# A decode block on one core: q, gate and up with x stationary in four column groups, and a new first and last DMA

## The chip, the core and the metric

The kernel runs on one core of a Trainium2 chip. The core has TensorE (PE, with its weight loads counted apart as PEld), VectorE (DVE), ScalarE (ACT), GpSimd (POOL) and SyncE (SP, which issues almost all DMAs here). The metric is the device time of one execution in microseconds (us). Three timed runs of the kernel before gave 197.55, 197.69 and 197.55 us, median 197.55.

## What is computed

One decode step of a gated mix of two branches that share the input x (4 rows of 512, bfloat16). Branch A is attention over the last 4096 positions of a cache, branch B is a gated feed-forward layer, and g is a scalar gate per row:

```python
g = sigmoid((x * gate_w).sum(-1, keepdims=True))
# A: 4 sequences, 32 query heads, 8 key/value heads of 128, window W = 4096 of 16384
q = (x @ wq).reshape(4, 1, 32, 128).transpose(0, 2, 1, 3)
k = repeat(k_cache[:, :, -4096:, :], 4, axis=1)        # v in the same way
p = softmax(einsum("bhqd,bhkd->bhqk", q, k) * 128 ** -0.5)
a = einsum("bhqk,bhkd->bhqd", p, v).reshape(4, 1, 4096) @ wo
# B: 512 -> 1792 -> 512
gate, up = x @ W_gate, x @ W_up
b = ((gate * (gate > 0)) * up) @ W_down
out = g * a + (1 - g) * b
```

All weights and caches are bfloat16. The window of both caches is 64 MB, wq and wo are 4 MB each, and the three matrices of B 1.75 MB each, so about 81 MB have to be read.

## The kernel before

The work on the cache is cut into eight sets (NSET): set s is sequence s // 2 and one half (four) of its key/value heads. A set's keys are one DMA of 4 MB into one of two buffers of Ksb (`load_k`, L235), its values one of 4 MB into one of two buffers of Vsb (`load_v`, L239). All big loads stand on SP's queue in one fixed order: wq, keys 0, then keys s and values s - 1 alternating, W_gate and W_up into the buffer that keys 6 leave free, values 7, W_down into the buffer of values 6, and wo in four pieces of 16, 10, 4 and 2 blocks (WO_CUTS) into the buffer that wq had. A load into a used buffer waits on SP for the last product that reads it, and all loads behind it wait with it. x and gate_w are two small loads on ACT's queue.

For a set, PE first transposes the keys in 16 groups of four 128x128 float32 blocks (two bfloat16 values as one; `kt`, L340), through three banks of PSUM (TR); each group is copied back to SBUF in bfloat16 by ACT (L345, nine of 16 groups) or DVE (L347). Then come the scores (`scores`, L373), with the query as the stationary operand of 32 columns and 512 keys as the moving one, in four column groups of the PE array, through three banks (SCB); DVE masks each bank of 512 columns and takes the maximum (L381). `maximum` reduces the maxima, `exponent` (ACT, L410) forms the weights, `turn` (DVE, L417) transposes them, `values` (PE, L429) multiplies them with the values into bank OB, whose result DVE copies to osb (L434); `combine` (PE, L442 and L445, then DVE to L450) adds the parts of the four column groups into bank FB, divides, multiplies by g and writes the set's columns of oq.

Every engine runs a list of operations in an order that is written out by hand (from L489). The class Program counts, for each operation, which semaphore values it has to wait for, and `emit` (L107) writes each engine's list into its own part of one `nc.Block()` (L562). For PE, sets 2 to 7 are three turns of a loop over one body of two sets. Block entry is a jump of every engine into its part; at its end the engines meet in a barrier.

The parts around the change. `qproj` (L454) runs first on PE, when wq has landed: for each of 32 heads, four products with a 128x128 block of wq stationary and the four columns of xT moving, into columns of FB; DVE casts the result (L461), two products with the matrices perm (made on POOL, L270) bring even and odd elements of a head apart (L464), and DVE spreads them into QS (L468), from which POOL copies a set's query to QSP (L357). `gateup` (L472) stands behind the exponents, `combine` of set 6 and the transpositions of set 7, and ahead of `values` of set 7: for each of 14 blocks of 128 and each of gate and up four products with a block of the weight stationary and xT moving (L477), into columns of FB; then three DVE operations (L481 to L483) form hT with the factor 1 - g. Last, PE multiplies hT with W_down (L545) and oq with wo (L553), both into bank AB in four column groups of 128 output columns; DVE copies AB to outs (L557), SP issues the DMA of the result, four rows of 128 columns from each of four places in outs (L558), and waits for it within the block (L559; the profile puts that wait at L562).

Of the kernel before, what the change touches and what calls it, by code (L numbers as in the profile page):

```python
# [5 lines left out]
FP32 = mybir.dt.float32  # L6
BF16 = mybir.dt.bfloat16
ACTF = mybir.ActivationFunctionType
ALU = mybir.AluOpType
# [4 lines left out]
HQ = 32  # L14
# [5 lines left out]
NSET = 8  # L20
NFT = FF // 128
# [12 lines left out]
class Program:  # L34
# [69 lines left out]
            if name is not None:  # L104
                ins.then_inc(sems[self.events[name][0]], step)

    def emit(self, engine, eng, sems):  # L107
        ops, plan = self.ops[engine], self.plan(engine)
        if engine != "pe":
            for op, need in zip(ops, plan):  # L110
                self.put(eng, sems, op, need)
            return
        n = len(self.turns) - 1
        base = []
# [38 lines left out]
def bass_gated_mix__sliding_block_cached__glu_gated_reglu__decode_kernel(  # L153
# [13 lines left out]
    with ExitStack() as ctx:  # L167
        def sb(name, shape, dt):
            return ctx.enter_context(nc.sbuf_tensor(name, shape, dt))
# [18 lines left out]
        qTb = sb("qTb", [128, 128], BF16)  # L188
        perm = sb("perm", [128, 2, 128], BF16)
# [15 lines left out]
        gtmp = sb("gtmp", [128, NFT * 4], FP32)  # L205
        gtmp2 = sb("gtmp2", [128, NFT * 4], FP32)
        hT = sb("hT", [128, NFT, 32], BF16)
        outs = sb("outs", [128, 128], BF16)
# [48 lines left out]
        wo_src = A_wo.rearrange("(p i) w -> p (i w)", p=128)  # L257
        for k in range(len(WO_CUTS) - 1):
            lo, hi = 512 * WO_CUTS[k], 512 * WO_CUTS[k + 1]
            P.dma("sp", lambda e, lo=lo, hi=hi: e.dma_start(Wbig[:, lo:hi], wo_src[:, lo:hi]), ("WO", k), [("Q",)])  # L260


        P.op("pool", lambda e: e.memset(ones[:, :], 1.0), ("ONES",))
# [5 lines left out]
        for h in range(2):  # L269
            P.op("pool", lambda e, h=h: e.affine_select(  # L270
                perm[:, h, :].rearrange("p (g k) -> p g k", g=2), ones[:, :].rearrange("p (g k) -> p g k", g=2),
                [[0, 2], [-2, 64]], ALU.is_equal, 0.0, base=-h, channel_multiplier=1), ("PERM", h), [("ONES",)])
        P.op("pool", lambda e: e.memset(m4[:, :], -NEG), ("M4Z",))
        for a in range(4):
            r = slice(32 * a, 32 * a + 32)
# [19 lines left out]
            ("WSUM",), [("S32", 3), ("WSEL", 3)])  # L295
        P.op("dve", lambda e: e.memset(QS[:, :, :].rearrange("p s w -> p (s w)"), 0.0), ("QZ",))
        P.op("dve", lambda e: e.memset(mcol[:, :], 0.0))
        P.op("dve", lambda e: e.memset(oq[:, :, :].rearrange("p i w -> p (i w)"), 0.0), ("OQZ",))
        P.op("dve", lambda e: e.memset(hT[:, :, :].rearrange("p i w -> p (i w)"), 0.0), ("HZ",))
        P.op("dve", lambda e: e.memset(mrow2[:, :], 0.0), ("M0",))  # L300
# [4 lines left out]
        for t in range(4):  # L305
# [2 lines left out]
        P.op("dve", lambda e: e.tensor_copy(xT[:, :].rearrange("p (t r) -> p t r", t=4)[:, :, 0:5],  # L308
                                            fbf[:, 0:32].rearrange("p (t r) -> p t r", t=4)[:, :, 0:5]),
             ("XTC",), [("XT",)])  # L310
        P.op("dve", lambda e: e.tensor_copy(gwB[:, :].rearrange("p (t m) -> p t m", t=4),
                                            xT[:, :].rearrange("p (t r) -> p t r", t=4)[:, :, 4:5].to_broadcast([128, 4, 128])),
             ("GWB",), [("XTC",)])
# [123 lines left out]
        def combine(s):  # L437
            par, b, half = s % 2, s // 2, s % 2
            r = slice(64 * half, 64 * half + 64)
            for k in range(8):  # L440
                lo = 3 - k % 4 + 64 * (k // 4)
                P.op("pe", lambda e, k=k, lo=lo: e.matmul(FB[r, 256:288], Wsel[:, lo:lo + 64], osb[:, par, 32 * k:32 * k + 32],  # L442
                                                          start=(k == 0), stop=(k == 7)), None,
                     [("OSB", s), ("WSUM",), ("QC", 1), ("G",), ("OQ", s - 1) if s >= 1 else None, ("H",) if s == NSET - 1 else None])
            P.op("pe", lambda e: e.matmul(FB[r, 288:288 + NPIECE], Wsum[:, :], rowsum[:, par, :], start=True, stop=True),  # L445
                 ("SUMS", s))
            P.op("dve", lambda e: e.tensor_reduce(ssum[r, par:par + 1], FB[r, 288:288 + NPIECE], AXIS.X, ALU.add),
                 ("SSUM", s), [("SUMS", s)])
            P.op("dve", lambda e: e.reciprocal(recip[r, par:par + 1], ssum[r, par:par + 1]), ("RECIP", s), [("SSUM", s)])
            P.op("dve", lambda e: e.tensor_scalar(oq[r, :, 8 * b], FB[r, 256:288], recip[r, par:par + 1],  # L450
                                                  gsb[r, b:b + 1], op0=ALU.mult, op1=ALU.mult),
                 ("OQ", s), [("RECIP", s), ("G",), ("OQZ",)])

        def qproj():  # L454
            for h in range(HQ):
                for t in range(4):
                    P.op("pe", lambda e, h=h, t=t: e.matmul(  # L457
                        FB[:, 64 + 4 * h:68 + 4 * h], Wq3[:, t, 128 * h:128 * h + 128], xT[:, t * 8:t * 8 + 4],
                        start=(t == 0), stop=(t == 3)),
                        ("Q",) if (h == HQ - 1 and t == 3) else None, [("WQ",), ("XTC",), ("G",)])  # L460
            P.op("dve", lambda e: e.tensor_copy(qTb[:, :].rearrange("p (b h) -> p b h", b=4),  # L461
                                                FB[:, 64:192].rearrange("p (h b) -> p b h", b=4)), ("QB",), [("Q",)])
            for h in range(2):
                P.op("pe", lambda e, h=h: e.matmul(OB[:, 128 * h:128 * h + 128], perm[:, h, :], qTb[:, :], start=True, stop=True),  # L464
                     ("QP",) if h == 1 else None, [("QB",), ("PERM", 1)])
            for g in range(2):
                r = slice(64 * g, 64 * g + 64)
                P.op("dve", lambda e, g=g, r=r: e.tensor_copy(  # L468
                    QS[r, :, 16 * g:16 * g + 16], OB[r, 0:256].rearrange("p (s j) -> p s j", j=16)),
                    ("QC", g), [("QP",), ("QZ",)])  # L470

        def gateup():  # L472
            for i in range(NFT):
                for which, W, key in ((0, Wg, "WG"), (1, Wu, "WU")):
                    col = 64 + 64 * which + 4 * i
                    for t in range(4):
                        P.op("pe", lambda e, W=W, i=i, t=t, col=col: e.matmul(  # L477
                            FB[:, col:col + 4], W[:, t, i:i + NFT * 127 + 1:NFT], xT[:, t * 8:t * 8 + 4],
                            start=(t == 0), stop=(t == 3)),
                            ("GU",) if (i == NFT - 1 and which == 1 and t == 3) else None, [("WG",), ("WU",), ("OQ", NSET - 2)])  # L480
            P.op("dve", lambda e: e.tensor_scalar(gtmp[:, :], FB[:, 64:64 + NFT * 4], 0.0, None, op0=ALU.max), ("H0",), [("GU",)])  # L481
            P.op("dve", lambda e: e.tensor_tensor(gtmp2[:, :], FB[:, 128:128 + NFT * 4], gtmp[:, :], ALU.mult), ("H1",), [("H0",)])
            P.op("dve", lambda e: e.tensor_tensor(  # L483
                hT[:, :, :].rearrange("p i (b o) -> p i b o", o=8)[:, :, :, 0], gtmp2[:, :].rearrange("p (i b) -> p i b", b=4),
                gsb[:, 4:8].rearrange("p (o b) -> p o b", o=1).to_broadcast([128, NFT, 4]), ALU.mult), ("H",),
                [("H1",), ("G",), ("HZ",)])


        qproj()  # L489
# [59 lines left out]
        for k in range(len(WO_CUTS) - 1):  # L549
            for i in range(WO_CUTS[k], WO_CUTS[k + 1]):  # L550
                for cb in range(4):
# [5 lines left out]
        P.op("dve", lambda e: e.tensor_copy(outs[:, :], AB[:, 0:128]), ("OUTS",), [("ACC",)])  # L557
        P.dma("sp", lambda e: e.dma_start(out.rearrange("b o (c d) -> c (b o) d", d=128), outs[0:128:8, :]), ("OUT",), [("OUTS",)])  # L558
        P.op("sp", None, None, [("OUT",)])  # L559

        sems = {name: ctx.enter_context(nc.semaphore(name)) for name in P.sems}
        with nc.Block() as block:  # L562
            @block.sync
            def _(e):
                P.emit("sp", e, sems)

            @block.gpsimd
            def _(e):
                P.emit("pool", e, sems)

            @block.tensor
            def _(e):
                P.emit("pe", e, sems)

            @block.vector
            def _(e):
                P.emit("dve", e, sems)

            @block.scalar
            def _(e):  # L580
                P.emit("act", e, sems)


# [26 lines left out]
```

## Time and profile before

The profiled execution took 197.38 us; its span, from the first to the last recorded instruction, is 195.7 us, and the mean granted clock of PE is 0.889 of full speed.

| | us in the span | share |
|---|---|---|
| PE products | 140.6 | 72% |
| PE weight loads | 107.7 | 55% |
| DVE | 103.6 | 53% |
| ACT | 91.5 | 47% |
| POOL | 7.9 | 4% |
| packets on SP's DMA queue (share of 16 DMA engines) | | 96.8% |

How the lines of the profile are read: a line of the chain has its start, its length and what it is; the chain is followed back from the end to what released each step. A line of the timeline has start, length, engine, line of the program, operation, the tiles written and read, the count of merged instructions, and in brackets the idle time ahead of it and what ended it. A line of the waits tells who waited for whom, in total, how often, and the longest. A line of a group has shortest, median and longest duration in nanoseconds, then first and last start. The forty digits are the busy share in forty equal slices of the span, in tenths. A line of the windows has the stretch and its length, the busy time of PE, PEld, DVE, ACT and POOL with the number of instructions, the granted clock of PE, the share of the 16 DMA engines that were busy, and GB/s.

### The profile page before, as it was taken

The numbers are of one execution on the slowest core, as the hardware profiler recorded it, in microseconds if no ns is written. First come the engines' busy times: TensorE is split into PE (matmuls) and PEld (weight loads), VectorE is DVE, ScalarE is ACT, GpSimd is POOL, SyncE is SP. The second block draws the span as 40 slices with busy tenths as digits, with TensorE's granted clock in tenths as the row PEclk, the third lists the DMA queues.
The fourth block names the chain that finished last, engine by engine and source line by source line (L and its number), as shares of the span: only waits on it lengthen the run. The fifth ranks groups of instructions, "written<-read, shape, count | busy, mean of one in ns | idle before, by whom it ended". The sixth has DMA issues, their size and how long they took to land.

```text
span 195.7 us, 4263 instructions
## 1 busy us (share of the span) xinstructions
PE 140.6 (72%) x1858; PEld 107.7 (55%) x1858; DVE 103.6 (53%) x278; ACT 91.5 (47%) x108; POOL 7.9 (4%) x39
## 2 busy tenths in 40 slices
PE   0134199968889919992999399929992999498634
PEld 0034197535567518751976286528752875397533
DVE  2102025888599456945585659456945584741200
ACT  2000058698398409760886098509750976220000
POOL 7400000000000000000000000000000000000000
PEclk9999999999999996997599879996996699965855
DMA  6999999999999999999999999999999999999991
GB/s 215 449 429 452 429 449 442 425 429 437 432 422 429 425 429 429 427 429 425 435 429 435 429 429 430 429 429 429 429 429 429 435 411 425 450 431 415 422 385 59
DMA packets 3498, 81.19 MB, mean 415 GB/s; under 512 B 409, under 2 KB 414, under 8 KB 670
## 3 DMA queue, kind: packets, MB, share of 16 engines
q1 hardware_dynamic: 3476, 81.01, 96.8%
q8 instruction: 9, 0.15, 0.3%
q14 instruction: 3, 0.02, 0.0%
q10 hardware_dynamic: 10, 0.01, 0.0%
HBM read 81.01 MB, written 0.00 MB: 414 GB/s over the span
## 4 chain that ended last, share of the span: by engine, by line
DMA 57%; PE 25%; ACT 9%; DVE 4%; issue 1%; SPq 1%
DMA Ksb<-in_A_k_cache_dram 46%; PE bank L340 16%; DMA Wbig<-in_A_wo_dram 12%; ACT Ksb L345 7%; PE bank L373 5%; DVE Ksb L347 2%; PE bank L429 2%; ACT sc L410 2%; PE bank L553 1%; PE bank L442 1%; DVE pT L417 1%; ACT L410 1%; DVE sc L381 1%; SPq L260 0%; DVE oq L450 0%
## 5 line engine op out<-in xcount | busy, mean ns | idle before, releaser
L345 ACT ACTIVATE Ksb<-bank 128x1024 bf16<-128x1024 bf16 x72 | 70.9, 1022 | 68.2 <-PE bank L340 68.0
L340 PE MATMUL bank<-identf,Ksb 128*128 128x128 f32 x512 | 81.1, 313 | 29.4 <-DMA Ksb<-in_A_k_cache_dram 24.0
L340 PEld LDWEIGHTS bank<-identf,Ksb 128*128 128x128 f32 x512 | 66.6, 161 | 44.1 <-DMA Ksb<-in_A_k_cache_dram 25.7
L347 DVE COPY Ksb<-bank 128x1024 bf16<-128x1024 bf16 x56 | 38.0, 685 | 41.8 <-PE bank L340 40.8
L381 DVE CUSTOM_DVE_ANT_0 sc<-bank,mask 128x512 bf16<-128x512 f32 x32 | 21.7, 684 | 9.6 <-PE bank L373 9.5
L429 PE MATMUL bank<-Vsb,pT 128*32 128x256 bf16 x512 | 20.8, 291 | 0.9 <-DMA Vsb<-in_A_v_cache_dram 0.9
L373 PE MATMUL bank<-Ksb,QSP 128*32 128x512 bf16 x256 | 19.4, 383 | 2.1 <-DVE Ksb L347 1.6
L410 ACT ACTIVATE sc<-sc,negmax 128x1024 bf16<-128x1024 bf16 x16 | 18.3, 1146 | 4.8 <-DVE negmax L402 4.7
L417 DVE STREAM_TRANSPOSE pT<-sc 128x1024 bf16<-128x1024 bf16 x16 | 19.7, 1237 | 1.3 <-ACT sc L410 1.0
L429 PEld LDWEIGHTS bank<-Vsb,pT 128*32 128x32 bf16 x512 | 13.2, 101 | 7.1 <-issue 3.3
L442 PEld LDWEIGHTS bank<-osb,Wsel 128*64 128x64 f32 x128 | 8.1, 138 | 4.6 <-issue 2.6
L442 PE MATMUL bank<-osb,Wsel 128*64 128x32 f32 x128 | 8.9, 224 | 1.2 <-DVE osb L434 1.2
L373 PEld LDWEIGHTS bank<-Ksb,QSP 128*32 128x32 bf16 x256 | 4.1, 94 | 9.4 <-DVE Ksb L347 4.4
L477 PE MATMUL bank<-xT,Ksb 128*128 128x4 bf16 x112 | 6.9, 199 | 1.8 <-DVE oq L450 1.8
L477 PEld LDWEIGHTS bank<-xT,Ksb 128*128 128x128 bf16 x112 | 6.8, 160 | 1.9 <-issue 1.9
L553 PE MATMUL bank<-Wbig,oq 128*32 128x128 bf16 x128 | 4.2, 311 | 4.1 <-DMA Wbig<-in_A_wo_dram 4.0
L357 POOL COPY QSP<-QS 128x64 bf16<-128x64 bf16 x8 | 1.8, 236 | 118.2 <-PE bank L373 107.4
L457 PE MATMUL bank<-xT,Wbig 128*128 128x4 bf16 x128 | 3.6, 166 | 4.0 <-DMA Wbig<-in_A_wq_dram 4.0
L306 PE MATMUL bank<-ident,xsb 5*128 5x5 bf16 x4 | 0.3, 167 | 7.9 <-DMA xsb<-in_gate_w_dram 7.9
L553 PEld LDWEIGHTS bank<-Wbig,oq 128*32 128x32 bf16 x128 | 3.1, 140 | 5.0 <-DMA Wbig<-in_A_wo_dram 5.0
L457 PEld LDWEIGHTS bank<-xT,Wbig 128*128 128x128 bf16 x128 | 3.5, 104 | 4.0 <-DMA Wbig<-in_A_wq_dram 4.0
L434 DVE COPY osb<-bank 128x256 f32<-128x256 f32 x8 | 3.4, 420 | 3.6 <-PE bank L429 3.6
(55 smaller groups left out, 47.0 us busy)
## 6 DMA issues: line engine op xcount, KB each, us to landing
Ksb<-in_A_k_cache_dram SPq DMA_DIRECT2D x8, 4096.0 KB, 22.9
Vsb<-in_A_v_cache_dram SPq DMA_DIRECT2D x8, 4096.0 KB, 32.0
Wbig<-in_A_wq_dram SPq DMA_DIRECT2D x1, 4096.0 KB, 12.2
Wbig<-in_A_wo_dram SPq DMA_DIRECT2D x1, 2048.0 KB, 20.2
Ksb<-in_B_W_gate_dram SPq DMA_DIRECT2D x1, 1792.0 KB, 17.9
Ksb<-in_B_W_up_dram SPq DMA_DIRECT2D x1, 1792.0 KB, 21.8
Vsb<-in_B_W_down_dram SPq DMA_DIRECT2D x1, 1792.0 KB, 15.6
Wbig<-in_A_wo_dram SPq DMA_DIRECT2D x1, 1280.0 KB, 22.8
```

The costliest lines, as they stand in the source:

```text
L340: P.op("pe", lambda e, bk=bk, cc=cc, c=c, s=s: e.transpose(bk[:, cc * 128:(cc + 1) * 128], kw[:, c * 128:(c + 1) * 128], identf[:, :]), (" ...
L345: P.op("act", lambda e: e.activation(dst, bk[:, :].bitcast(BF16), ACTF.Copy), ("KTC", s, i), [("KT", s, i)])
L347: P.op("dve", lambda e: e.tensor_copy(dst, bk[:, :].bitcast(BF16)), ("KTC", s, i), [("KT", s, i)])
L373: P.op("pe", lambda e, a=a, h=h: e.matmul(bk[32 * a:32 * a + 32, 0:512], QSP[:, s % 2, h, :], k4[:, 16 * bank:16 * bank + 16, 32 * a:32 * ...
L381: P.op("dve", lambda e: e.tensor_tensor_reduce(sc[:, s % 2, bank * 512:(bank + 1) * 512], bk[:, :], mask[:, :], 1.0, LOWEST, ALU.add, ALU.max,
L410: P.op("act", lambda e: e.activation(sc[:, par, k * PW:(k + 1) * PW], sc[:, par, k * PW:(k + 1) * PW], ACTF.Exp, bias=negmax[:, par:par + ...
L417: P.op("dve", lambda e: e.transpose(pT[:, par, k * PW:(k + 1) * PW], sc[:, par, k * PW:(k + 1) * PW]), ("PTT", s, k), [("EXP", s, k), ("PV ...
L429: P.op("pe", lambda e, c=c, g=g, col=col: e.matmul(OB[32 * g:32 * g + 32, 0:256], pT[:, par, col:col + 32], v3[:, 16 * k + c, :], start=(k ...
L442: P.op("pe", lambda e, k=k, lo=lo: e.matmul(FB[r, 256:288], Wsel[:, lo:lo + 64], osb[:, par, 32 * k:32 * k + 32], start=(k == 0), stop=(k ...
L457: P.op("pe", lambda e, h=h, t=t: e.matmul(FB[:, 64 + 4 * h:68 + 4 * h], Wq3[:, t, 128 * h:128 * h + 128], xT[:, t * 8:t * 8 + 4], start=(t ...
L477: P.op("pe", lambda e, W=W, i=i, t=t, col=col: e.matmul(FB[:, col:col + 4], W[:, t, i:i + NFT * 127 + 1:NFT], xT[:, t * 8:t * 8 + 4], star ...
L553: P.op("pe", lambda e, i=i, cb=cb: e.matmul(AB[32 * cb:32 * cb + 32, 0:128], oq[:, i, :], Wo3[:, i, cb * 128:(cb + 1) * 128], start=False, ...
```

## The change

- The first DMA of SP (wq) is issued ahead of the block, and SP's last operation, the wait for the result's DMA, behind it. `emit` gets bounds lo and hi for that.
- q: xP holds xT's four columns of x beside 28 zero columns, for each quarter t of the contraction. Each product has xP stationary (32 columns) and 512 columns of wq moving, in four column groups: 32 products into two banks of SCB. DVE copies the first bank twice into qdup, ACT the second; 16 products with qdup stationary and four columns of the identity moving bring q into the old layout in OB. The matrices perm go.
- gate and up: in the same way, 448 columns a group, 16 products each into two banks of TR; three passes and a transposition of 32x32 blocks on DVE form hT. PE waits for the banks of TR, no longer for FB, and `combine` of the last set no longer waits for H.
- A row of the result sits in rows 0 to 3 of a column group, no longer in every eighth row. Four copies (two on DVE, two on ACT) put the groups beside each other in outs, 4 rows of 512, and the result's DMA is a plain one of four rows.

```diff
-    def emit(self, engine, eng, sems):
+    def emit(self, engine, eng, sems, lo=0, hi=None):
...
-            for op, need in zip(ops, plan):
+            for op, need in list(zip(ops, plan))[lo:hi]:
...
+        P.op("dve", lambda e: e.tensor_copy(xP[:, :, 0:4], xT[:, :].rearrange("p (t r) -> p t r", t=4)[:, :, 0:4]),
+             ("XP",), [("XTC",), ("XZ",)])
...
-                     [("OSB", s), ("WSUM",), ("QC", 1), ("G",), ("OQ", s - 1) if s >= 1 else None, ("H",) if s == NSET - 1 else None])
+                     [("OSB", s), ("WSUM",), ("QC", 1), ("G",), ("OQ", s - 1) if s >= 1 else None])
...
         def qproj():
-            for h in range(HQ):
+            for n in range(2):
                 for t in range(4):
-                    P.op("pe", lambda e, h=h, t=t: e.matmul(
-                        FB[:, 64 + 4 * h:68 + 4 * h], Wq3[:, t, 128 * h:128 * h + 128], xT[:, t * 8:t * 8 + 4],
-                        start=(t == 0), stop=(t == 3)),
...
+                    for g in range(4):
+                        j = 4 * n + g
+                        P.op("pe", lambda e, n=n, t=t, g=g, j=j: e.matmul(
+                            SCB[n][32 * g:32 * g + 32, 0:512], xP[:, t, :], Wq3[:, t, 512 * j:512 * j + 512],
+                            start=(t == 0), stop=(t == 3), tile_position=(0, 32 * g)),
+                            ("Q", n) if (t == 3 and g == 3) else None, [("WQ",), ("XP",), ("G",)])
+            for n in range(2):
+                src = SCB[n][:, :].rearrange("p (m k c) -> p m c k", m=4, c=2)
+                for o in range(2):
+                    if n == 0:
+                        P.op("dve", lambda e, n=n, o=o, src=src: e.tensor_copy(qdup[:, n, :, :, o, :], src),
+                             ("QB", n, o), [("Q", n)])
+                    else:
+                        P.op("act", lambda e, n=n, o=o, src=src: e.activation(qdup[:, n, :, :, o, :], src, ACTF.Copy),
+                             ("QB", n, o), [("Q", n)])
...
+                        P.op("pe", lambda e, n=n, c=c, m=m: e.matmul(
+                            to[:, c, :, n, :, m], qdup[:, n, m, c, :, :].rearrange("p o k -> p (o k)"), of_b,
+                            start=True, stop=True),
...
         def gateup():
-            for i in range(NFT):
-                for which, W, key in ((0, Wg, "WG"), (1, Wu, "WU")):
...
+            for bank, W, key in ((TR[0], Wg, "WG"), (TR[1], Wu, "WU")):
+                for t in range(4):
+                    for g in range(4):
+                        P.op("pe", lambda e, bank=bank, W=W, t=t, g=g: e.matmul(
+                            bank[32 * g:32 * g + 32, 0:448], xP[:, t, :], W[:, t, 448 * g:448 * g + 448],
+                            start=(t == 0), stop=(t == 3), tile_position=(0, 32 * g)),
+                            ("GU", key) if (t == 3 and g == 3) else None,
+                            [(key,), ("KTC", NSET - 1, 14), ("KTC", NSET - 1, 15)])
...
+            P.op("dve", lambda e: e.transpose(gtmp3[:, :, :].rearrange("p i l -> p (i l)"),
+                                              gtmp2[:, :, :].rearrange("p i l -> p (i l)")), ("H2",), [("H1",)])
...
-        P.op("dve", lambda e: e.tensor_copy(outs[:, :], AB[:, 0:128]), ("OUTS",), [("ACC",)])
-        P.dma("sp", lambda e: e.dma_start(out.rearrange("b o (c d) -> c (b o) d", d=128), outs[0:128:8, :]), ("OUT",), [("OUTS",)])
+        for c in range(4):
+            to, src = outs[0:4, 128 * c:128 * c + 128], AB[32 * c:32 * c + 4, 0:128]
+            if c % 2 == 0:
+                P.op("dve", lambda e, to=to, src=src: e.tensor_copy(to, src), ("OUTS", c), [("ACC",)])
+            else:
+                P.op("act", lambda e, to=to, src=src: e.activation(to, src, ACTF.Copy), ("OUTS", c), [("ACC",)])
+        P.dma("sp", lambda e: e.dma_start(out.rearrange("b o d -> (b o) d"), outs[:, :]), ("OUT",), [("OUTS", c) for c in range(4)])
...
+        P.emit("sp", nc.sync, sems, 0, 1)
         with nc.Block() as block:
             @block.sync
             def _(e):
-                P.emit("sp", e, sems)
+                P.emit("sp", e, sems, 1, -1)
...
+        P.emit("sp", nc.sync, sems, -1)
```

More of the change, by code (lines that the diff above doesn't have):

```diff
@@ L187, in bass_gated_mix__sliding_block_cached__glu_gated_reglu__decode_kernel @@
         gsb = sb("gsb", [128, 8], FP32)
-        qTb = sb("qTb", [128, 128], BF16)
-        perm = sb("perm", [128, 2, 128], BF16)
+        qdup = sb("qdup", [128, 2, 4, 2, 2, 64], BF16)
+        xP = sb("xP", [128, 4, 32], BF16)
         QS = sb("QS", [128, 2 * NSET, 32], BF16)
@@ L204, in bass_gated_mix__sliding_block_cached__glu_gated_reglu__decode_kernel @@
         oq = sb("oq", [128, 32, 32], BF16)
-        gtmp = sb("gtmp", [128, NFT * 4], FP32)
-        gtmp2 = sb("gtmp2", [128, NFT * 4], FP32)
+        gtmp = sb("gtmp", [128, 32, NFT], FP32)
+        gtmp2 = sb("gtmp2", [128, NFT, 32], FP32)
+        gtmp3 = sb("gtmp3", [128, NFT, 32], FP32)
         hT = sb("hT", [128, NFT, 32], BF16)
-        outs = sb("outs", [128, 128], BF16)
+        outs = sb("outs", [4, 512], BF16)
         banks = [ctx.enter_context(nc.psum_tensor("bank%d" % i, [128, 512], FP32)) for i in range(8)]
@@ L259, in bass_gated_mix__sliding_block_cached__glu_gated_reglu__decode_kernel @@
             lo, hi = 512 * WO_CUTS[k], 512 * WO_CUTS[k + 1]
-            P.dma("sp", lambda e, lo=lo, hi=hi: e.dma_start(Wbig[:, lo:hi], wo_src[:, lo:hi]), ("WO", k), [("Q",)])
+            P.dma("sp", lambda e, lo=lo, hi=hi: e.dma_start(Wbig[:, lo:hi], wo_src[:, lo:hi]), ("WO", k), [("Q", 1)])
         P.op("pool", lambda e: e.memset(ones[:, :], 1.0), ("ONES",))
@@ L268, in bass_gated_mix__sliding_block_cached__glu_gated_reglu__decode_kernel @@
                                                base=0, channel_multiplier=1), ("IDENTF",), [("ONESF",)])
[L269 to L272, printed above, removed]
         P.op("pool", lambda e: e.memset(m4[:, :], -NEG), ("M4Z",))
@@ L297, in bass_gated_mix__sliding_block_cached__glu_gated_reglu__decode_kernel @@
         P.op("dve", lambda e: e.memset(mcol[:, :], 0.0))
+        P.op("dve", lambda e: e.memset(xP[:, :, :].rearrange("p t w -> p (t w)"), 0.0), ("XZ",))
         P.op("dve", lambda e: e.memset(oq[:, :, :].rearrange("p i w -> p (i w)"), 0.0), ("OQZ",))
@@ L449, in combine @@
             P.op("dve", lambda e: e.reciprocal(recip[r, par:par + 1], ssum[r, par:par + 1]), ("RECIP", s), [("SSUM", s)])
-            P.op("dve", lambda e: e.tensor_scalar(oq[r, :, 8 * b], FB[r, 256:288], recip[r, par:par + 1],
+            P.op("dve", lambda e: e.tensor_scalar(oq[r, :, b], FB[r, 256:288], recip[r, par:par + 1],
                                                   gsb[r, b:b + 1], op0=ALU.mult, op1=ALU.mult),
@@ L454, in qproj @@
         def qproj():
-            for h in range(HQ):
+            for n in range(2):
                 for t in range(4):
-                    P.op("pe", lambda e, h=h, t=t: e.matmul(
-                        FB[:, 64 + 4 * h:68 + 4 * h], Wq3[:, t, 128 * h:128 * h + 128], xT[:, t * 8:t * 8 + 4],
-                        start=(t == 0), stop=(t == 3)),
-                        ("Q",) if (h == HQ - 1 and t == 3) else None, [("WQ",), ("XTC",), ("G",)])
-            P.op("dve", lambda e: e.tensor_copy(qTb[:, :].rearrange("p (b h) -> p b h", b=4),
-                                                FB[:, 64:192].rearrange("p (h b) -> p b h", b=4)), ("QB",), [("Q",)])
@@ L463, in qproj @@
-            for h in range(2):
-                P.op("pe", lambda e, h=h: e.matmul(OB[:, 128 * h:128 * h + 128], perm[:, h, :], qTb[:, :], start=True, stop=True),
-                     ("QP",) if h == 1 else None, [("QB",), ("PERM", 1)])
+                    for g in range(4):
[4 more added lines that the diff above has]
+                            ("Q", n) if (t == 3 and g == 3) else None, [("WQ",), ("XP",), ("G",)])
@@ new lines, in qproj @@
+            of_b = ident[:, :].rearrange("p (g w) -> p w g", g=4)[:, 0:4, :]
+            to = OB[:, 0:256].rearrange("p (c b n g m) -> p c b n g m", c=2, b=4, n=2, g=4)
+            for n in range(2):
+                for c in range(2):
+                    for m in range(4):
+                        P.op("pe", lambda e, n=n, c=c, m=m: e.matmul(
+                            to[:, c, :, n, :, m], qdup[:, n, m, c, :, :].rearrange("p o k -> p (o k)"), of_b,
+                            start=True, stop=True),
+                            ("QP",) if (n, c, m) == (1, 1, 3) else None, [("QB", n, 1), ("IDENT",)])
@@ L472, in gateup @@
         def gateup():
-            for i in range(NFT):
-                for which, W, key in ((0, Wg, "WG"), (1, Wu, "WU")):
[L475 to L480, printed above, removed]
@@ L481, in gateup @@
-            P.op("dve", lambda e: e.tensor_scalar(gtmp[:, :], FB[:, 64:64 + NFT * 4], 0.0, None, op0=ALU.max), ("H0",), [("GU",)])
-            P.op("dve", lambda e: e.tensor_tensor(gtmp2[:, :], FB[:, 128:128 + NFT * 4], gtmp[:, :], ALU.mult), ("H1",), [("H0",)])
-            P.op("dve", lambda e: e.tensor_tensor(
-                hT[:, :, :].rearrange("p i (b o) -> p i b o", o=8)[:, :, :, 0], gtmp2[:, :].rearrange("p (i b) -> p i b", b=4),
-                gsb[:, 4:8].rearrange("p (o b) -> p o b", o=1).to_broadcast([128, NFT, 4]), ALU.mult), ("H",),
-                [("H1",), ("G",), ("HZ",)])
+            for bank, W, key in ((TR[0], Wg, "WG"), (TR[1], Wu, "WU")):
[6 more added lines that the diff above has]
+                            [(key,), ("KTC", NSET - 1, 14), ("KTC", NSET - 1, 15)])
@@ new lines, in gateup @@
+            P.op("dve", lambda e: e.tensor_scalar(gtmp[:, :, :].rearrange("p l i -> p (l i)"), TR[0][:, 0:448], 0.0, None,
+                                                  op0=ALU.max), ("H0",), [("GU", "WG")])
+            P.op("dve", lambda e: e.tensor_tensor(
+                gtmp2[:, :, :].rearrange("p i l -> p l i"), TR[1][:, 0:448].rearrange("p (l i) -> p l i", i=NFT),
+                gtmp[:, :, :], ALU.mult), ("H1",), [("H0",), ("GU", "WU")])
+            P.op("dve", lambda e: e.transpose(gtmp3[:, :, :].rearrange("p i l -> p (i l)"),
+                                              gtmp2[:, :, :].rearrange("p i l -> p (i l)")), ("H2",), [("H1",)])
@@ L489, in bass_gated_mix__sliding_block_cached__glu_gated_reglu__decode_kernel @@
+            P.op("dve", lambda e: e.tensor_tensor(
+                hT[:, :, 0:4], gtmp3[:, :, 0:4], gsb[:, 4:8].rearrange("p (o b) -> p o b", o=1).to_broadcast([128, NFT, 4]),
+                ALU.mult), ("H",), [("H2",), ("G",), ("HZ",)])
         qproj()
```

## The prediction

> **What bounds the kernel now.** I read the page's forty slices first, then the queue shares, the chain, and the two ends.
>
> ```profile
> DMA  6999999999999999999999999999999999999991
> q1 hardware_dynamic: 3476, 81.01, 96.8%
> q8 instruction: 9, 0.15, 0.3%
> HBM read 81.01 MB, written 0.00 MB: 414 GB/s over the span
> ```
>
> The 16 DMA engines are full in every slice but the first and last. Nothing that only shortens an engine's work in the middle can pay. The last pieces of the chain agree:
>
> ```profile
> 168.06 22.77 DMA Wbig<-in_A_wo_dram
> 190.83 0.04 issue
> 190.87 1.85 PE bank L553 x56
> 192.72 0.01 issue
> 192.74 0.43 PE bank L553 x8
> 193.17 0.02 issue
> 193.19 0.29 DVE outs L557
> ```
>
> The last wo pieces arrive; 8 products, one copy and the output's DMA follow. So a gain can come from three places: an earlier first byte, an earlier end of the stream, a shorter stretch from 192.7 on. The DMA columns of the windows show how the stream ends (second column from the end: busy share):
>
> ```profile
> 189.00:190.00 1.00, 0.70 (x28) 0.43 (x18) 0.00 (x0) 0.00 (x0) 0.00 (x0) 0.50 0.99 406
> 190.00:191.00 1.00, 0.13 (x8) 0.13 (x12) 0.00 (x0) 0.00 (x0) 0.00 (x0) 0.50 0.68 272
> 191.00:192.00 1.00, 1.00 (x40) 0.86 (x34) 0.00 (x0) 0.00 (x0) 0.00 (x0) 0.50 0.58 219
> 192.00:193.00 1.00, 0.99 (x32) 0.49 (x24) 0.00 (x0) 0.00 (x0) 0.00 (x0) 0.50 0.04 14
> ```
>
> From 191 to 192 only 0.58 of 16, some nine engines, still work. Following the trace's packet records engine by engine (each packet starts where its engine's previous one ended), seven engines end at 190.2 to 190.8 and nine at 191.7 to 192.28. The late ones are those that carried an instruction fetch: a 16 KB packet of q8 holds an engine 1.0 to 1.07 us, and the 32 KB packet behind it takes some 1.7 instead of 1.21, so about 1.5 us each. Six of the nine fetches can be placed (at 19.6, 38.1, 52.5, 64.5, 80.0 and 91.2), on six different engines, all late. One fetch on one engine is what sets the stream's end.
>
> The tail, from the timeline and the groups of the block's end:
>
> ```profile
> 193.51 0.69 SPq L558 DMA_DIRECT2D out_dram<-outs  x1
> ...
> SPq L562 <- DMA out_dram<-outs: 1.1, 1, 1.1
> ...
> L562 SPq COMPARE_BRANCH x1: 32/32/32, 195.3 to 195.3; - x1
> ...
> L562 PEldq EVENT_SEMAPHORE  x1: 51/51/51, 195.6 to 195.6; - x1
> ```
>
> SP starts the output's DMA at 193.51, its packets move from 194.81 to 194.93 (packet records), SP passes its wait at 195.28, and then a barrier of all engines runs to 195.66.
>
> **The reference for the sum.** The profiled execution took 197.38 us, 195.7 of it span and 1.68 around it. The median of the three timed runs is 197.55, 0.17 above. I sum differences in the span and put them on 197.55.
>
> **Head.** SP passes the start barrier at 0.743 and issues wq at 0.81; between lies its jump into the block. Issued ahead of the block, wq starts up to 0.07 earlier. First packets come 1.02 after the issue and nothing else holds them. Taken: -0.07 (bounds -0.09 and 0). x's two loads stay on ACT's queue and may now stand behind wq's first packets (1.6 to 2.1 us each): xT is ready at 8.34, the products wait for wq's landing at 13.0, so 4 us cover that. SP's other issues keep their order; k0 is not needed before 23.86.
>
> **q.** Removed: 128 products (3.58), the cast (0.29), two permuting products (0.40). Added: a small memset and copy for xP (0.09 to 0.43, beside the wait for wq), 32 products of 512 columns in four column groups, four 128x512 copies, 16 products of 4 columns. By the scores' row (8 such products in 0.62) the 32 cost 2.5, at half clock 5.0. The two DVE copies lie between 2x0.42 (256 columns, L434) and 2x0.69 (512 with a mask, L381); the two on ACT are below 2x1.02 (L345); the 16 products cost 16x0.028=0.45; QC and QSP stay (0.88, 0.41). From 13.0 that gives 18.1 to 21.2, against 18.83 now. What covers it is PE's wait for k0, to 23.86; the scores that need q start at 34.85. Taken: 0. Without that cover it would cost up to 2.4. The POOL operations that go (0.54) lie before 7.6, waited for by nobody in time. The four wo loads wait for Q, long past when SP comes to them at 167.6.
>
> **Gate and up.** Removed: 112 products (6.87, from 170.92 to 177.79) and three DVE operations (0.85). Added: 32 products, 2.2 (448 of 512 columns of the scores' row) to 4.4 at half clock, from about 169.1 (W_up has landed at 168.8), so done by 173.5. On DVE behind the transposes that end at 173.64: two passes over 448 columns at 0.42 to 0.69, a 32x32 transposition of 448 float32 columns at 0.6 to 1.24 (half or all of L417's row), and 0.41: done by 176.7 at the latest. PE goes on at 178.69 either way:
>
> ```profile
> 178.69 3.60 PE L429 MATMUL bank<-Vsb,pT 128*32 128x256 bf16 x64 [0.91 <-DMA Vsb<-in_A_v_cache_dram]
> ```
>
> So the 4 to 6 us become idle time before V's landing. hT is needed at 183.97, osb's copy (next on DVE) at 182.35: nothing queued behind is late. The Trainium skill speaks against this edit: its page "TensorEngine Tiling (Array Packing)", section PSUM Bottleneck, says that tiled products move the cost to PSUM's evacuation. The rows agree (56 columns now, 448 then); with the rule or without, the sum is 0 here. The combination of the last set no longer waits for H (ready at 178.73, needed at 182.83): 0.
>
> **Instruction fetches.** PE's fetches come after 281, 497, 790, 1015, 1284 and 1531 of its recorded instructions, one per 250 or so. The change has 162 products fewer, each with its weight load: 324 fewer of some 2300 instructions in program order. Of the fetches that land before the stream's end (eight now) seven or so remain. One is enough to hold an engine to 192, so the end stays: taken 0. Bounds: -0.5 if those left fall on engines that started early (first packets end between 3.68 and 4.22), +1.5 if two fall on one engine. The Trainium skill's page "Runtime: NRT & Kernel Launch", section Instruction fetch mechanics, calls the crossing of a block "mostly hidden" and says that a jump outside a two-page window fetches the page anew. The trace differs on both: each fetch costs its engine 1.5 us of a full stream, and PE's loop jumps back over 740 instructions at 88.9 and 127.9 with no q8 packet between 91.2 and 177.8. By the page's first rule the fetches are worth 0, by the row also, as long as one is left.
>
> **Tail.** The one copy (0.292) becomes two on DVE and two on ACT. DVE: two of 0.29 in a row with 0.03 between (as the pair of L468, 0.417 at 0.448 apart) end 0.32 later. ACT: 128 columns lie between 0.17 (4 columns, L318) and 1.02 (1024, L345), by the line through both 0.28, the second 0.17 behind, so 0.45: DVE ends last. SP waits for two engines instead of one: 0.05, an estimate from its barrier step of 0.04. Together +0.37 (bounds +0.1 and +0.5).
>
> The output's DMA: four rows of 1 KB in place of 16 pieces of 256 B. Its issue took 0.695, packets came 1.30 after its start. The same four rows of 1 KB are in the trace as x's load: packets 0.96 after the start, and 1.02 for wq. That saves 0.28 to 0.34; the packets themselves 0.06. Taken -0.35; bounds -0.45 and -0.1 (x's issue of 0.56 with the output's own 0.60 from issue to packets).
>
> The barrier: now drains and barrier stand behind SP's wait, 195.28 to 195.66. With the wait behind the block they run while the DMA is under way (issued by 194.2, landed a microsecond later), and the program ends with the wait. -0.35 (bounds -0.40 and, if the runtime's own end waits for something else, 0). Nothing is queued behind the waiting SP.
>
> **Sum.** -0.07 + 0.37 - 0.35 - 0.35 = -0.40, and the last 8 products may find a faster clock (granted 0.50 now; 0.43 would be 0.25 at most faster): I take -0.1 of it. -0.5 on 197.55 gives 197.05.
>
> **The rivals**, against a bound of 0.2% (0.4 us), about what a measurement of this kernel can tell from no change.
> - *The tail's own work eats the gain*: copies and wait at +0.5, the DMA at -0.1, barrier and head at -0.3: +0.1 to -0.3, so 197.25 to 197.65. For: the four copies are certain, the DMA's saving rests on a load, not a store. Against: x's row has the very same four pieces. 0.22.
> - *A second fetch on one engine* (slower): place, the engine that ends last; price 1.5, so 198.0 to 198.6; it decides from +0.9 on. For: fetch times move, the loop's body moves by 164 instructions across the blocks of 256 and spans four of them instead of three, so it may be refetched. Against: six placed fetches on six engines, none in the second and third pass. 0.13.
> - *The stream ends earlier*, its fetches on early starters and one fewer: a further -0.3 to -0.5, so 196.3 to 196.75. 0.10.
> - *The change doesn't do it*: the wait behind the block brings nothing since the runtime waits longer elsewhere: 197.4. 0.05.
>
> **How the numbers follow.** Forecast 0.50, 196.75 to 197.4. Faster (below 197.15): 0.42 of the forecast and the 0.10 = 0.52. Same: 0.08 + 0.22 + 0.05 = 0.35. Slower 0.13. The range leaves out most of the slow rival (0.11) and the lower half of the early end (0.05): 196.5 to 198.0.
>
> **What the profile after would show.** wq's issue at 0.74; q's products from 13 and QSP before 22; PE idle from 173 to 178.7; seven or so q8 packets and about nine engines busy in the last microsecond of the stream; two DVE copies over 0.6 us; packets of the output 1.0 behind its issue; barrier lines before the last landing. Wrong it would be if V's landing no longer came last at 178.7, if q8 grew, or if the output's DMA took as long as now.

## The result and the profile after

The changed kernel takes 196.42 us (median of 6 runs, 196.29 to 197.04) against 197.61 of the kernel before (6 runs, 197.50 to 198.00). The ratio is 0.9944, with a 95% interval of 0.9928 to 0.9960: faster by 0.56%, some 1.1 us. A second series of 5 runs gave 0.9948 (0.9935 to 0.9960). The forecast was 197.05 with a range of 196.5 to 198.0: the direction came, the gain is about twice the forecast's 0.5 us, and the median lies just below the range's lower end.

The profiled execution took 196.39 us, its span is 195.2. So 0.99 us went from one profiled execution to the other (197.38 before), but only half of it from the span (195.66 to 195.15 to the hundredth); the other half went from what lies around the span, 1.72 before and 1.24 now (1.68 and 1.19 by the rounded spans).

The page of the changed kernel (slices and queues):

```profile
DMA  6999999999999999999999999999999999999992
q1 hardware_dynamic: 3464, 81.01, 97.1%
q8 instruction: 8, 0.13, 0.3%
HBM read 81.01 MB, written 0.00 MB: 415 GB/s over the span
```

The stream is as full as before and carries the same bytes, with one 16 KB instruction packet fewer (queue q8). The windows at its end, the second column from the right being the busy share of 16 DMA engines:

```profile
190.00:191.00 1.00, 0.10 (x8) 0.10 (x12) 0.00 (x0) 0.00 (x0) 0.00 (x0) 0.50 0.66 256
191.00:192.00 1.00, 1.00 (x40) 0.89 (x39) 0.00 (x0) 0.00 (x0) 0.00 (x0) 0.50 0.46 180
192.00:193.00 1.00, 1.00 (x32) 0.49 (x24) 0.00 (x0) 0.00 (x0) 0.00 (x0) 0.50 0.02 8
```

Fewer engines are late from 191 to 192 (a share of 0.46, some seven of the 16, instead of 0.58, some nine), but some still are. The trace also holds a record of each DMA packet, with its queue, size, start and duration; by these the last byte of wo comes at 192.24, against 192.28. The last pieces of the chain start at the same places as before, too:

```profile
190.85 0.04 issue
190.90 1.83 PE bank L572 x56
192.72 0.00 issue
192.73 0.43 PE bank L572 x8
193.16 0.02 issue
193.19 0.28 DVE outs L579
193.47 0.32 DVEq L587
```

Up to 193.19, where the first copy of the result starts, nothing has been won. All that the change brings lies behind it. The timeline from there, and the groups of the block's end (L587) and of the waits that SP executes as instructions of their own (L101):

```profile
193.19 0.56 ACT L581 ACTIVATE outs<-bank 4x128 bf16<-4x128 f32 x2 [20.53 <-PE bank L572]
193.19 0.60 DVE L579 CAST outs<-bank 4x128 bf16<-4x128 f32 x2 [7.45 <-PE bank L572]
193.84 0.35 SPq L582 DMA_DIRECT2D out_dram<-outs  x1
```

```profile
L587 SPq DRAIN  x1: 167/167/167, 194.2 to 194.2; - x1
L587 SPq EVENT_SEMAPHORE  x1: 17/17/17, 194.6 to 194.6; - x1
...
L587 PEldq EVENT_SEMAPHORE  x1: 51/51/51, 194.6 to 194.6; - x1
...
L101 SPq EVENT_SEMAPHORE  x2: 17/17/17, 193.8 to 195.1; - x2
```

The issue of the result's DMA took 0.35 instead of 0.69. The barrier at the block's end is over at 194.62 (195.66 before), and SP's last wait, now behind it, at 195.15.

### The profile page after: what moved, and what is told of

Read it like the earlier page. It is cut to its first block, busy times and chain, and to the rows that moved or that the text cites. A ratio compares the mean times of both kernels' runs of the same rounds, so it can differ in the third digit from the quotient of the medians.

```text
span 195.2 us, 3947 instructions
## 1 busy us (share of the span) xinstructions
PE 138.4 (71%) x1696; PEld 101.0 (52%) x1696; DVE 107.0 (55%) x283; ACT 93.2 (48%) x112; POOL 7.4 (4%) x37
## 4 chain that ended last, share of the span: by engine, by line
DMA 57%; PE 30%; ACT 9%; DVE 2%; issue 1%; SPq 1%; DVEq 0%
DMA Ksb<-in_A_k_cache_dram 46%; PE bank L340 19%; DMA Wbig<-in_A_wo_dram 12%; ACT Ksb L345 7%; PE bank L373 6%; PE bank L429 2%; PE bank L442 2%; DVE Ksb L347 1%; ACT sc L410 1%; PE bank L572 1%; ACT L410 1%; SPq L261 0%; SPq L246 0%; SPq L256 0%; DVEq L587 0%
## 5 line engine op out<-in xcount | busy, mean ns | idle before, releaser
L373 PE MATMUL bank<-Ksb,QSP 128*32 128x512 bf16 x256 | 20.0, 394 | 2.0 <-DVE Ksb L347 1.6
L442 PEld LDWEIGHTS bank<-osb,Wsel 128*64 128x64 f32 x128 | 8.8, 148 | 5.1 <-issue 3.1
L442 PE MATMUL bank<-osb,Wsel 128*64 128x32 f32 x128 | 9.7, 233 | 1.2 <-DVE osb L434 1.2
L581 ACT ACTIVATE outs<-bank 4x128 bf16<-4x128 f32 x2 | 0.5, 270 | 20.6 <-PE bank L572 20.5
L459 PE MATMUL bank<-Wbig,xP 128*32 128x512 bf16 x32 | 3.5, 616 | 3.8 <-DMA Wbig<-in_A_wq_dram 3.8
L402 DVE TENSOR_SCALAR negmax<-mall 32x1 f32<-32x1 f32 x32 | 4.6, 144 | 1.0
L388 DVE TENSOR_REDUCE mq<-mx 32x1 f32<-32x4 f32 x32 | 4.6, 143 | 0.8
```

The source lines that it names most:

```text
L373: P.op("pe", lambda e, a=a, h=h: e.matmul(bk[32 * a:32 * a + 32, 0:512], QSP[:, s % 2, h, :], k4[:, 16 * bank:16 * bank + 16, 32 * a:32 * ...
L388: P.op("dve", lambda e, a=a: e.tensor_reduce(mq[:, a:a + 1], mx[32 * a:32 * a + 32, par, :], AXIS.X, ALU.max), ("MAXQ", s, a), [("SCC", s, ...
L402: P.op("dve", lambda e, a=a: e.tensor_scalar(negmax[32 * a:32 * a + 32, par:par + 1], mall[:, 0:1], -SCALE, None, op0=ALU.mult), ("NEGMAX" ...
```

## The experiments

**What makes the time: the end of the span, or the barrier.** Theory A was the prediction's: a fixed 1.7 us follows the last recorded instruction. Theory B was formed on the changed kernel's 1.19: the time ends some 1.75 us after the barrier at the block's end. Four kernels were to tell them apart. The first is the kernel before with the wait alone behind the block:

```diff
-                P.emit("sp", e, sems)
+                P.emit("sp", e, sems, 0, -1)
...
                 P.emit("act", e, sems)
+        P.emit("sp", nc.sync, sems, -1)
```

> The kernel before with one edit: SP's last wait stands behind the block. Theory A (the time ends a fixed 1.7 us after the last recorded instruction, so only the barrier behind the landing is saved): 0.35 us less, ratio 0.998. Theory B (the time ends about 1.75 us after the barrier at the block's end, since the runtime's own end on the other engines follows that barrier and SP's wait for the landing runs beside it): the barrier moves from 195.66 to 194.6, about 1.0 us less, ratio 0.995, and the time around the span falls from 1.68 to about 1.1.

Measured: 196.81 us, ratio 0.9964 (0.9951 to 0.9978), 0.7 us less; 1.36 to 1.45 around the span in all five runs. Neither theory's number: twice A's 0.35, some three quarters of B's 1.0. The groups of the block's end show why it is less than B:

```profile
L562 SPq DRAIN  x1: 423/423/423, 194.5 to 194.5; - x1
L562 SPq EVENT_SEMAPHORE  x1: 17/17/17, 195.1 to 195.1; - x1
...
L562 PEldq EVENT_SEMAPHORE  x1: 51/51/51, 195.1 to 195.1; - x1
```

Behind the issue of sixteen pieces SP's drain lasts 0.42 (0.17 behind the four pieces of the changed kernel), and the barrier ends only at 195.14. 195.14 and 1.72 make 196.86, which is what this execution took.

The second is the changed kernel with the wait back in the block:

```diff
-                P.emit("sp", e, sems, 1, -1)
+                P.emit("sp", e, sems, 1)
...
-        P.emit("sp", nc.sync, sems, -1)
```

> The changed kernel with one edit undone: SP's last wait is back inside the block. Landing at 195.13, barrier to about 195.5. Theory A: 0.35 us more than the changed kernel, so 0.8 less than before (ratio 0.996). Theory B: 195.5 plus 1.72, 0.85 us more than the changed kernel, so 0.2 to 0.3 less than before (ratio 0.9985), and the time around the span is back at 1.7.

Measured: 197.40 us, ratio 0.9991 (0.9982 to 1.0000). That is near B's 0.9985; A's 0.996 lies outside the interval. All but 0.2 us of the gain is gone with this one edit, and the median time around the span is back at 1.76. In the block, SP's wait again comes ahead of the barrier:

```profile
L587 SPq COMPARE_BRANCH  x1: 33/33/33, 195.5 to 195.5; - x1
...
L587 PEldq EVENT_SEMAPHORE  x1: 51/51/51, 195.8 to 195.8; - x1
```

The third sends the result's DMA, too, from behind the block:

```diff
-                P.emit("sp", e, sems, 1, -1)
+                P.emit("sp", e, sems, 1, -2)
...
-        P.emit("sp", nc.sync, sems, -1)
+        P.emit("sp", nc.sync, sems, -2)
```

> The changed kernel with the result's DMA itself, not its wait alone, behind the block. The barrier no longer waits for SP's issue (ends near 194.05 instead of 194.62), the issue comes 0.3 later, the landing near 195.4 instead of 195.13. Theory A: 0.3 us more than the changed kernel (ratio to before 0.996). Theory B: up to 0.55 less (ratio to before 0.9915), unless SP's own end then comes last.

Measured: 196.99 us, ratio 0.9965 (0.9951 to 0.9979). The barrier ends at 194.13, half a microsecond earlier than in the changed kernel, and SP's wait at 195.51:

```profile
L587 PEldq EVENT_SEMAPHORE  x1: 51/51/51, 194.1 to 194.1; - x1
```

```profile
194.20 0.35 SPq L582 DMA_DIRECT2D out_dram<-outs  x1
```

The time did not fall with the barrier; it rose with SP's wait, as A had it (0.996). In four of five runs 1.21 to 1.29 lie around the span.

The fourth makes SP wait longer:

```diff
         P.op("sp", None, None, [("OUT",)])
+        P.dma("sp", lambda e: e.dma_start(spare[:, :], A_x.rearrange("b o d -> (b o) d")), ("SPARE",))
+        P.op("sp", None, None, [("SPARE",)])
```

> The changed kernel, and behind its last wait SP loads four rows of x once more into a spare tile and waits for them (1.3 to 1.5 us; a repeated load that nothing uses). Theory A: the time ends with SP, 1.3 to 1.5 us more than the changed kernel. Theory B: the runtime's end on the other engines covers part of it: by how much less than 1.4 the time grows is the slack that SP's wait had.

Measured: 197.91 us, ratio 1.0016 (1.0007 to 1.0026), 1.5 us more than the changed kernel, with 1.19 to 1.29 around a span of 196.7. The added load is 1.4 us of SP's time, and SP's last wait is over 1.67 later than in the changed kernel's profile, of which 0.35 is a later end of the stream:

```profile
194.15 0.35 SPq L583 DMA_DIRECT2D out_dram<-outs  x1
195.44 0.26 SPq L585 DMA_DIRECT2D spare<-in_A_x_dram  x1
```

So SP's wait had next to no slack in the changed kernel, and B alone falls as A alone did. What fits most of the profiled executions is model M: **the time is the later of the barrier's end plus 1.72 and SP's last wait plus 1.22.** The 1.72 was read off the kernel before, where the barrier decides, the 1.22 off the executions of the changed kernel, where SP's wait lies higher by a hair; the other rows test them:

| profiled execution | barrier's end | SP's last wait | model M | time |
|---|---|---|---|---|
| before | 195.66 | 195.61 | 197.38 | 197.38 |
| changed | 194.62 | 195.15 | 196.37 | 196.39 |
| changed, second series | 194.84 | 195.37 | 196.59 | 196.61 |
| wait alone behind | 195.14 | 195.52 | 196.86 | 196.86 |
| copies and DMA alone | 195.66 | 195.62 | 197.38 | 197.38 |
| SP waits longer | 194.93 | 196.82 | 198.04 | 198.06 |
| old result, wait behind | 194.96 | 195.35 | 196.68 | 196.68 |
| PE's loop written out | 195.84 | 196.38 | 197.60 | 197.62 |
| two queues | 195.38 | 195.72 | 197.10 | 197.24 |
| last piece of one block | 195.09 | 195.62 | 196.84 | 197.00 |

Eight of these ten rows lie within 0.02 of the model, two some 0.15 above it. In three further profiled executions (wait back inside, DMA behind, q, gate and up alone) the time is 0.4 to 0.9 above it; the last section comes back to all five. What happens in the 1.72 and 1.22, of which a part may lie ahead of the first recorded instruction, is outside the records. So the model is a fit to these runs and not a seen mechanism. That the place of the wait makes the gain does not rest on it: the first two kernels show that by their times.

**The parts alone.** The kernel before with the four copies and the plain DMA:

```diff
-        P.op("dve", lambda e: e.tensor_copy(outs[:, :], AB[:, 0:128]), ("OUTS",), [("ACC",)])
...
+            if c % 2 == 0:
+                P.op("dve", lambda e, to=to, src=src: e.tensor_copy(to, src), ("OUTS", c), [("ACC",)])
...
+        P.dma("sp", lambda e: e.dma_start(out.rearrange("b o d -> (b o) d"), outs[:, :]), ("OUT",), [("OUTS", c) for c in range(4)])
```

> The kernel before with the four small copies and the plain DMA of four rows of 1 KB; the wait stays inside the block, q, gate and up as before. By the changed kernel's trace the copies end 0.30 later and the landing comes 1.30 after the issue instead of 1.77: 0.15 to 0.2 less (ratio 0.999) by both theories. If the stretch between were different without the other edits: up to 0.3 more.

Measured: 197.46 us, ratio 0.9996 (0.9987 to 1.0005), not to be told from no change. Measured from the last product's end, which leaves the stream's scatter out, the tail of the profiled execution is 4.09 instead of 4.24, the 0.15 that was expected.

The new q, gate and up alone, with the old head and tail:

```diff
-            for h in range(HQ):
+            for n in range(2):
                 for t in range(4):
+                    for g in range(4):
...
-            for i in range(NFT):
-                for which, W, key in ((0, Wg, "WG"), (1, Wu, "WU")):
+            for bank, W, key in ((TR[0], Wg, "WG"), (TR[1], Wu, "WU")):
```

> The new q, gate and up with the old first DMA, the old single copy, the old DMA of sixteen pieces and the wait inside the block. Theory: all of it lies in PE's waits for k0 and for the last values, and the stream's end is held by engines with one instruction fetch, of which seven are left: 0, ratio 0.999 to 1.001. Rival: fewer fetches end the stream earlier: 0.3 to 0.5 less, ratio 0.998, with the last wo piece before 192.0.

Measured: 197.65 us, ratio 1.0003 (0.9994 to 1.0012). Nothing. The timeline of the changed kernel shows where the shorter products went:

```profile
169.30 1.70 PE L491 MATMUL bank<-Ksb,xP 128*32 128x448 bf16 x32
...
173.86 0.58 DVE L496 TENSOR_SCALAR gtmp<-bank 128x448 f32<-128x448 f32 x1
174.48 0.91 DVE L498 TENSOR_TENSOR gtmp<-bank,gtmp 128x448 f32<-128x448 f32 x1
175.42 0.65 DVE L501 STREAM_TRANSPOSE gtmp<-gtmp 128x448 f32<-128x448 f32 x1
...
178.67 3.61 PE L429 MATMUL bank<-Vsb,pT 128*32 128x256 bf16 x64 [7.67 <-DMA Vsb<-in_A_v_cache_dram]
```

PE is through with gate and up at 171.0 instead of 177.8 and then waits 7.67 us for the last values, which land at the same time as before.

The changed kernel with the old single copy and sixteen pieces (the four copies and the plain DMA, whose diff is shown further up, taken back):

> The changed kernel with the single copy and the DMA of sixteen pieces of the kernel before; first DMA ahead of the block, wait behind it, q, gate and up as changed. Model M (the time is the later of: the barrier's end plus 1.72, and SP's last wait plus 1.22): the long issue (0.69) and SP's drain behind it (0.42 in the run with the wait alone) hold the barrier to 195.1, so 196.8, 0.45 more than the changed kernel, and the landing near 195.4 is not what ends. Rival (the copies and the DMA are worth 0.1 to 0.15 as they were with the wait inside): 196.55.

Measured: 196.79 us, ratio 0.9960 (0.9947 to 0.9973), beside 0.9948 of the changed kernel on the same chip: 0.2 us, nearer to the rival. The 0.45 was a slip in the expectation, not in M: it set side by side two executions whose streams ended 0.26 apart (192.50 with the wait alone, 192.24 in the changed kernel). Counted from the last product's end, M gives 3.48 against 3.24, and the profiled executions took 3.48 and 3.26.

**The stream's end and the instruction fetches.** The changed kernel with PE's loop written out:

```diff
-        if engine != "pe":
+        if True:
```

> The changed kernel with PE's loop over sets 2 to 7 written out: the same products in the same order, some 1400 more instructions in the program, so 13 or 14 instruction fetches on q8 before the stream's end instead of 7. Theory F (each fetch falls on another engine and the stream ends with any engine that had one): 0, ratio to the changed kernel 0.999 to 1.001, stream's end near 192.2, nearly all engines late instead of nine. Rival G (fetches meet on one engine): 1.5 us more. Rival H (the end follows the total of fetches, 1.5 us times 6 or 7 over 16 engines): 0.6 more.

Measured: 197.94 us, ratio 1.0019 (1.0010 to 1.0028): 1.5 us more than the changed kernel. Same products, same order, same data bytes; the page shows 13 packets of q8 instead of 8, and the windows a later end:

```profile
q8 instruction: 13, 0.21, 0.4%
```

```profile
191.00:192.00 1.00, 0.00 (x0) 0.00 (x0) 0.00 (x0) 0.00 (x0) 0.00 (x0) 0.50 0.62 238
192.00:193.00 1.00, 0.91 (x36) 0.91 (x40) 0.00 (x0) 0.00 (x0) 0.00 (x0) 0.50 0.33 131
193.00:194.00 1.00, 0.98 (x36) 0.48 (x28) 0.00 (x0) 0.00 (x0) 0.00 (x0) 0.50 0.09 33
```

Twelve of the 13 fetches begin by 185, the last one at 191.88. Theory F (another engine each time) falls: from 191 to 192 only a share of 0.62 of the 16 engines is late, a third go on to 193, and the last byte comes at 193.48, 1.24 later. By the packet records at least five engines are done by 190.8, as those without a fetch were in the kernel before, while some four are still at work at 193.2; in the other twelve profiled executions no engine loads beyond 192.61. That is what G says: two fetches meet on one engine, and the stream ends with it. The records do not name the engine of a packet, so the meeting is worked out from these ends and not seen. H's 0.6 is too little.

**Two other ends, tried for a faster version.** The result in two halves over two queues:

```diff
+        P.op("dve", lambda e: e.tensor_copy(outs[0:64, :], AB[0:64, 0:128]), ("OUTS", 0), [("ACC",)])
+        P.op("act", lambda e: e.activation(outs[64:128, :], AB[64:128, 0:128], ACTF.Copy), ("OUTS", 1), [("ACC",)])
+        P.dma("sp", lambda e: e.dma_start(cols[0:2], outs[0:64:8, :]), ("OUT", 0), [("OUTS", 0)])
+        P.dma("act", lambda e: e.dma_start(cols[2:4], outs[64:128:8, :]), ("OUT", 1), [("OUTS", 1)])
```

> The changed kernel, the result in another way: DVE copies two column groups in one operation and ACT the other two (0.29 in place of two in a row), and each half is sent by a DMA of its own, eight pieces of 256 B, one on SP's queue, one on ACT's. Model M: copies end 0.30 earlier; if eight pieces are issued in 0.46, landing near 194.95 and barrier near 194.5: 196.2, 0.2 less than the changed kernel. If ACT's issue takes 0.56 and its drain 0.4 as SP's with sixteen: barrier 194.9, so 196.6, 0.2 more.

Measured: 197.03 us, ratio 0.9975 (0.9966 to 0.9984), 0.4 worse than the changed kernel. The copies did end 0.3 earlier, but either issue took as long as that of sixteen pieces, and both drains behind them grew:

```profile
193.73 0.64 ACTq L580 DMA_DIRECT2D out_dram<-outs  x1
193.74 0.67 SPq L579 DMA_DIRECT2D out_dram<-outs  x1
```

```profile
L585 ACTq DRAIN  x1: 748/748/748, 194.4 to 194.4; - x1
L585 SPq DRAIN  x1: 696/696/696, 194.5 to 194.5; - x1
```

The last piece of wo cut smaller:

```diff
-WO_CUTS = (0, 16, 26, 30, 32)
+WO_CUTS = (0, 16, 26, 31, 32)
```

> The changed kernel with the last piece of wo cut from two blocks to one, so four products instead of eight behind the last landing: 0.1 less than the changed kernel if the landing stays (0.43 for eight, 0.29 for a first wave of four), 0 if the wave of eight is as long as that of four.

Measured: 196.66 us, ratio 0.9949 (0.9936 to 0.9962), no difference to the changed kernel's 196.61. The piece ahead of the last, now five blocks, came so late that 24 products instead of 8 stood behind 192.77:

```profile
192.77 0.83 PE L572 MATMUL bank<-Wbig,oq 128*32 128x128 bf16 x24 [0.28 <-DMA Wbig<-in_A_wo_dram]
```

What these two and the old result with the wait behind are compared with is the changed kernel once more, on their chip:

> The changed kernel itself on the chip of the other three, as what they are compared with: ratio 0.9944 as before, span near 195.2 and 1.21 around it by model M.

Measured: 196.61 us, ratio 0.9948 (0.9935 to 0.9960), span 195.3 to 195.4 and 1.24 around it. None of the versions tried beats it; by model M its two ends are level (194.62 and 1.72 make 196.34, 195.15 and 1.22 make 196.37), so shortening one of them alone would bring at most a few hundredths.

## Why the prediction was right in direction and half in size

- **What bounds the kernel.** Right. The stream ends at 192.24, and the gain lies wholly behind 193.19.
- **Head (-0.07).** It did not come. SP issues wq at 0.804 instead of 0.811. The step failed where the jump into the block was taken for the whole of the 0.07 between barrier and issue: 0.06 of it is there without the jump as well. Its bound of 0 was the value.
- **q (0).** Right, and shown by the kernel with these parts alone, which took as long as the kernel before. The 32 products took 3.49, within the bounds of 2.5 and 5.0; q's query tile was ready 0.7 later than before, against k0 as cover. k0 itself came earlier: PE began on it at 22.79 instead of 23.90, and the first fetch of PE's program, at 19.6 before, came only at 32.8. (In the three kernels with the old q PE begins between 23.90 and 24.26, with a fetch at 18.7 to 19.6; in all with the new q between 22.79 and 23.23, with none before 31.7. The two go together in all 13 profiled executions; that the fetch is the cause was not tried by itself.) One microsecond was won there and did nothing for the end, since the stream goes on.
- **Gate and up (0).** Right; PE's products end 2.5 earlier than the bound, DVE's operations at 176.3, under the bound of 176.7. The Trainium skill ("TensorEngine Tiling (Array Packing)", PSUM Bottleneck) warns that after such a speed-up the copy out of PSUM may become the bottleneck. The rows show the shift: PE's 6.87 became 1.70, DVE's 0.85 became 2.36. It costs nothing here because the wait for the values covers both.
- **Instruction fetches (0; -0.5 to +1.5).** Right in size: seven before the end instead of eight, and the end stayed, with some seven engines late instead of the nine that were expected. The written-out loop shows that fetches are not free in a full stream: 13 instead of 8 in the span, 1.5 us more, as much as the prediction's upper bound. The Trainium skill ("Runtime: NRT & Kernel Launch", Instruction fetch mechanics) calls the cost of a crossing mostly hidden; these runs differ. The refetch of the loop's body that the slow rival named did not happen: no q8 packet between 88.5 and 182.2.
- **Copies and result DMA (+0.37 and -0.35).** The copies end 0.30 later and SP's second wait costs 0.03, a little less than summed. The DMA was undersized: its issue fell from 0.695 to 0.348, and from its start to SP's wake-up it takes 1.30 instead of 1.77, so -0.47, just past the bound of -0.45. x's load, an issue of 0.56, was not the nearest row: wq's issue on SP's own queue, 0.39, was. Together -0.14 instead of +0.02, and 0.15 in the kernel that had this alone.
- **Barrier (-0.35).** This is the term that was mis-sized: by the profiled executions it was worth -0.84. The prediction moved the barrier off the end of the span and kept the 1.68 around the span as a constant; its bounds (-0.40 and 0) allowed for a runtime that takes the gain away, not for one that adds to it. The barrier's end moved by 1.04, from 195.66 to 194.62, and what follows it at 1.72 moved with it, until SP's last wait, with 1.22 behind it, took over at the same height. The kernel with the wait alone behind the block gains 0.7, and the changed kernel with the wait back inside keeps 0.2 of its gain.
- **PE's clock (-0.1).** Did not come: the granted clock is 0.50 in the last stage in both, and the last eight products take 0.43 in both. The prediction had no row for it and should have left it out.

The sum by the terms as measured, on the profiled executions: head and stream -0.01, copies and DMA -0.14, and the rest, -0.84, by the wait that went behind the barrier. That the median came as near to the range as 0.1 is luck: the low end of the range was drawn for another rival, an earlier end of the stream, which did not come.

## What to carry to other kernels

In a kernel that ends like this one, the wait for the last DMA belongs behind the barrier that ends the block, where the other engines do not wait with it; its worth is not the barrier's own time (0.35) but all that hangs on the barrier, outside the span too (0.7 alone). So a sum should be made for the whole time, and what lies around the span be asked for a cause like any other term. In this kernel, whose DMA engines are all full, shorter products were worth nothing, and the length of the program was part of the traffic.

## What the runs showed beyond that

- The drain behind the issue of the result's DMA was not the same everywhere: 0.17 behind four pieces of 1 KB, 0.42 behind sixteen of 256 B, 0.70 (SP) and 0.75 (ACT) where two queues issue eight pieces each at the same time. Eight pieces on each of two queues took as long to issue (0.64 and 0.67) as sixteen on one (0.69).
- Some executions take longer around the span without a longer span: in the profiled ones of three kernels it was 2.1 to 2.5 us instead of 1.2 to 1.8. In these three the last 16 KB instruction packet begins long after the block's end (197.65, 196.97 and 197.00), in the other profiled kernels at 194.5 or earlier. The two rows that lie 0.15 above model M (two queues, last piece of one block) are odd in the same place: their records hold no such packet after 189.0, while the eight that fit the model have their last one between 191.8 and 194.5. They go together here; that the packet is the cause was not tried.
- With seven or eight instruction fetches ahead of its end, the stream ended between 192.24 and 192.61 in twelve profiled executions. With 13 it ended at 193.48, though five engines or more were done by 190.8. So fetches seem to meet on one engine before each engine has had one. How an engine is chosen is not in the records.
